# Wider transposes of the probabilities in a fused attention and gated-MLP kernel

## The chip, the cores and the metric

One Trainium2 chip, one of its NeuronCores. The metric is device time in microseconds (us) of one execution. Three runs of the kernel before gave 1160.24 us in the median (1160.02 to 1163.11).

## What is computed

The reference is local attention over 8 batches, 8 heads, 576 positions and 64 dimensions, followed by a gated MLP on 4608 tokens:

```python
scores = scale * np.matmul(q, k.transpose(0, 1, 3, 2))
masks = np.stack([mask_plain if h < H // 2 else mask_dil for h in range(H)], axis=0)
attn = softmax(np.where(masks, scores, -1e9))       # 32 keys back; heads 4 to 7: every 4th key, 128 back
x = np.matmul(attn, v)                              # (8 batches x 576) tokens x 512
xn = x / rms * rms_g
g = xn @ w_gate                                     # 512 -> 1536
out = (g * sigmoid(g) * (xn @ w_val)) @ w_out       # 1536 -> 512
```

## The kernel before, in words

The tokens are cut into 16 units of 288. A unit has 4 pairs of heads. In two of them the queries come in 3 blocks of 96 (QB); in the two dilated pairs they come in 4 blocks of 72, one for each residue class. So a unit has 14 blocks (a "burst" each), 6 with 96 queries and 8 with 72, and each block holds two heads.

A block passes through these steps, each on its own engine. PE multiplies queries and keys (`scored`, L452 in the first two units, L455 later). VectorE (DVE) adds the mask and takes the row maximum into the tile `t` (`scores_max`, L332 and L337). ScalarE (ACT) exponentiates in place (L347). DVE reduces and inverts the sums (L354, L355). GpSimd (POOL) scales the rows in place (L357; DVE for a part of unit 0). Then PE transposes the probabilities, once for each of the two heads (`transposed`, L429). In that transpose the probabilities are the stationary operand and an identity matrix of as many columns as the block has queries is the moving one: 96 or 72 columns. ACT and DVE take the result out of PSUM (`untranspose`, L412 and L414), and PE multiplies it with the values (`output`, L438, or L443 and L444).

The tile `t` comes from a rotating pool with 3 buffers under the tag "t". Every fourth block of the first two units takes a tile under the tag "qs" instead (L329, L330).

The transposed probabilities have no PSUM bank of their own. A bank holds 512 fp32 columns; the gate and value products of the MLP use 288 of them (U), and `gate` and `val` hand on the columns from U to U + 2*QB (L631, L657), and `products` takes them as `t_ps`.

The MLP runs over 12 slices (NJ) of the hidden size for every unit. One slice is three steps: the gate product (12 matmuls, L588 to L590, three for each of 4 chunks since both operands are split into a high and a low fp32r part), the value product (12 matmuls) and the projection of the slice before (12 matmuls). In units 0 and 1 the attention is in plain fp32, and unit 0 has its MLP in plain fp32 too (L585), while the weights are still decoded from fp64 bits on DVE and split (L152 to L162).

The order is written out by hand. `plan` puts each block's scores, transpose and output at a step of the main loop; in a step, PE first gets the MLP matmuls and then, by `attend`, the transposes, outputs and scores that fall on it. Work of the other engines is put off by a number of steps with a rank (`later`, `flush`). A unit's attention runs during the MLP of the unit before it. The transposes stand five steps after their block's scores, and the output two or three steps after the transpose. In the opening, before the first MLP step, each step also gets three or seven dummy matmuls (`busy`, L700).

At the very start POOL fills constants: the identity (`make_identity`), masks, sums (L97) and the zero halves of the first query and key tiles (L223).

Of the kernel before, what the change touches and what calls it, by code (L numbers as in the profile page):

```python
# [9 lines left out]
F32 = mybir.dt.float32  # L10
# [10 lines left out]
P = 128  # L21
U = S // 2
NU = NT // U
W = 32
DIL = 4
QB = 96
NC = DM // P
NJ = FF // P
NNAT = 2
# [35 lines left out]
def attn_moe(ctx: ExitStack, tc: tile.TileContext, qk_in, v_in, w_gate, w_val, w_out, rms_g, outT):  # L65
# [3 lines left out]
    nc = tc.nc  # L69
    V, A, G, PE = nc.vector, nc.scalar, nc.gpsimd, nc.tensor  # L70

    cst = ctx.enter_context(tc.tile_pool(name="cst", bufs=1))
    sb = ctx.enter_context(tc.tile_pool(name="sb", bufs=2))
    ps = ctx.enter_context(tc.tile_pool(name="ps", bufs=1, space=PSUM))


    ident = cst.tile([QB, QB], F32, name="ident")
    make_identity(nc, ident)
    one = cst.tile([P, 1], F32, name="one")
    G.memset(one, 1.0)  # L80
    ones = cst.tile([P, P], F32R, name="ones")
# [9 lines left out]
    G.affine_select(out=mask, in_=mask, pattern=[[1, P]], compare_op=ALU.is_ge,  # L91
                    fill=BIG, base=-1, channel_multiplier=-1)
    gs = cst.tile([P, NC], F32, name="gs")

    sums = [cst.tile([QB, 2, 4], F32, name=f"sum{k}") for k in range(5)]
    for sm in sums:
# [225 lines left out]

    st, xraw, xsq = {}, {}, {}

    def scores_max(u, c, i, s_ps):
        blocks, nq, _ = geometry(u, c)
        _, _, mc, n = blocks[i]
        sv = s_ps[:QB].rearrange("q (a t k) -> q a t k", a=2, t=2)
        other = u < NNAT and everything.index((u, c, i)) % 4 == 3  # L329
        t = sb.tile([QB, 2, P], F32, tag="qs" if other else "t", name=f"t_{u}_{c}_{i}", bufs=3)  # L330
        if u >= NNAT:
            V.tensor_tensor(out=t[:nq, :, :n], in0=sv[:nq, :, 1, :n],  # L332
                            in1=mask[:nq, None, mc:mc + n].to_broadcast([nq, 2, n]), op=ALU.add)
        sm = sums[everything.index((u, c, i)) % len(sums)]
        for a in range(2):
            plus = t[:nq, a, :n] if u >= NNAT else mask[:nq, mc:mc + n]
            V.tensor_tensor_reduce(out=t[:nq, a, :n], in0=sv[:nq, a, 0, :n], in1=plus,  # L337
                                   op0=ALU.add, op1=ALU.min, scale=-1.0 / math.sqrt(D),
                                   scalar=3e38, accum_out=sm[:nq, a, 0:1])
        st[u, c, i] = t, sm  # L340
# [75 lines left out]
    def products(q, t, o, t_ps, s_tag="s", o_tag="o"):  # L416


        if q:
            s_ps = ps.tile([P, 512], F32, tag=s_tag, name=f"s_{q[0]}_{q[1]}_{q[2]}")  # L420
        if o:
            o_ps = ps.tile([P, 512], F32, tag=o_tag, name=f"o_{o[0]}_{o[1]}_{o[2]}")
            pt = st.pop(o)
        if t:
            p, _ = st.pop(t)
        def transposed(a):
            blocks, nq, _ = geometry(*t[:2])
            n = blocks[t[2]][3]
            PE.transpose(t_ps[:n, a * QB:a * QB + nq], p[:nq, a, :n], ident[:nq, :nq])  # L429

        def output(a):
            blocks, nq, _ = geometry(*o[:2])
            n = blocks[o[2]][3]
            if a:
                return
            out = o_ps[:, :2 * nq].rearrange("d (a q) -> d a q", a=2)
            if o[0] < NNAT:
                PE.matmul(out, vs.pop(o)[:n].rearrange("k a d -> k (a d)"), pt[:n, 0, :, :nq], start=True, stop=True)  # L438
                return
            vh, vl = (part[:n].rearrange("k a d -> k (a d)") for part in vparts[everything.index(o) % 2])  # L440

            both = o_ps[:, :4 * nq].rearrange("d (t a q) -> d t a q", t=2, a=2)
            PE.matmul(both, vh, pt[:n, :, :, :nq], start=True, stop=False)  # L443
            PE.matmul(out, vl, pt[:n, 0, :, :nq], start=False, stop=True)  # L444

        def scored(a):
            blocks, nq, _ = geometry(*q[:2])
            qc, kc, _, n = blocks[q[2]]
            sv = s_ps[:QB].rearrange("q (a t k) -> q a t k", a=2, t=2)
            if q[0] < NNAT:  # L450
                qk = heads[q[0], 2 * q[1] + a]
                PE.matmul(sv[:nq, a, 0, :n], qk[:, qc:qc + nq], qk[:, U + kc:U + kc + n], start=True, stop=True)  # L452
                return
            qs, ks = heads[q[0], 2 * q[1] + a]
            PE.matmul(sv[:nq, a, :, :n], qs[:, qc:qc + nq], ks[:, :, kc:kc + n], start=True, stop=True)  # L455

        parts = [(b, fn, a) for b, fn in ((t, transposed), (o, output), (q, scored)) for a in range(2)]
        for b, fn, a in parts:
            if b:
                fn(a)  # L460
        if t:
            later(1, 0.2, lambda: untranspose(t, t_ps))
        if o:
            later(1, 0.5, lambda: take(*o, o_ps))
            if o[0] >= NNAT:
                later(1, 4, lambda: add(*o, o_ps))
            if o[0] < NNAT:
                later(1, 9, lambda: load_v(further(o, 3)))
            far = further(o, 2)
            if far and far[0] >= NNAT:  # L470
                split_v(far, 8 if o[0] < NNAT else 1)
        if q:
            later(1, 0.7, lambda: scores_max(*q, s_ps))
            later(2, 2, lambda: scores_exp(*q))
            later(3 if q[0] < NNAT else 4, -1, lambda: scores_norm(*q))
            u, c, i = q
            nxt = after(u, 2 * c, 2)
            nb = len(geometry(u, c)[0])
            if u < NNAT:
                if u == NNAT - 1 and c == NC - 1 and i == nb - 1:  # L480
                    for a in range(2):
                        later(1, 9, lambda a=a: load(NNAT, a))
                        later(5 + a, 9, lambda a=a: split(NNAT, a, (1, 2, 2, 3), G, V))
            elif nxt and i == 0:
                split(*nxt, (1, 2, 2, 3), G, V)
                split(nxt[0], nxt[1] + 1, (2, 3, 3, 4), G, V)
# [91 lines left out]
    hs, acc, gv = {}, {}, {}  # L578
# [30 lines left out]
    def gate(u, j):  # L609
        g_ps = group("g", u, j)  # L610
        if u == 0:
            used.append(("g", j))
        g = g_ps[:, :U]

        def tanh():
            nonlocal g
            t = (sb.tile([P, U], F32, tag="hhi", name=f"h_{j}", bufs=2) if u == 0 else
                 sb.tile([P, U], F32, tag="th", name=f"th_{u}_{j}", bufs=1))
            if u + j == 0:
                g = sb.tile([P, U], F32, tag="hhi", name="g_first", bufs=2)  # L620
                V.tensor_tensor(out=g, in0=g_ps[:, :U], in1=root[0], op=ALU.mult)
            A.activation(out=t, in_=g, func=AF.Tanh, scale=0.5)  # L622
            gv[u, j] = t

        def silu():
            t = gv[u, j]
            V.scalar_tensor_tensor(out=t, in0=t, scalar=1.0, in1=g, op0=ALU.add, op1=ALU.mult)  # L627

        later(1, 0 if u + j else 0.65, tanh)
        later(1, 0.8, silu)  # L630
        return g_ps[:, U:U + 2 * QB]  # L631

    def val(u, j):
        v_ps = group("v", u, j)
        if u == 0:
            used.append(("v", j))

        def prod():
            t = gv[u, j]
            V.tensor_tensor(out=t, in0=t, in1=v_ps[:, :U], op=ALU.mult)  # L640
            if u + j == 0:
                V.tensor_tensor(out=t, in0=t, in1=root[0], op=ALU.mult)

        def parts():
            t = gv.pop((u, j))
            if u == 0:
                hs[u, j] = t
                return
            hi = sb.tile([P, U], F32R, tag="hhi", name=f"hhi_{u}_{j}", bufs=2)
            lo = late[0].tile([P, U], F32R, tag="hlo", name=f"hlo_{u}_{j}", bufs=2)  # L650
            A.copy(out=hi, in_=t)  # L651
            G.tensor_tensor(out=lo, in0=t, in1=hi, op=ALU.subtract)  # L652
            hs[u, j] = (hi, lo)

        later(1 if u + j else 2, 0, prod)
        later(1 if u + j else 2, 0.5, parts)
        return v_ps[:, U:U + 2 * QB]  # L657

    def proj(u, j):
        if u == 0:  # L660
# [70 lines left out]
    for n in range(ends):  # L731
        decode(STEPS[n])
        flush()
        t_ps = None
        if "t" in events.get(n, {}):
            t_ps = ps.tile([P, 512], F32, tag="gv"[n % 2], name=f"t_first_{n}")[:, :2 * QB]
        attend(t_ps, s_tag=("s", "acc0", "acc1")[n % (3 if n < nb else 2)], o_tag=("o", "acc2")[n % 2])
        if n < nb + LAG:
            busy(BUSY[1])
        for kind, c in FIRST.get(n, ()):  # L740
            start(kind, c)
        if n == ends - 1:
            _, v_free = gate(0, 0), val(0, 0)
        now[0] += 1
# [101 lines left out]
```

## Time and profile before

| | us |
|---|---|
| median of 3 runs | 1160.24 |
| lowest and highest | 1160.02, 1163.11 |
| the profiled execution, its own time | 1162.36 |
| its span in the trace | 1160.6 |
| PE busy | 1125.2 (97%) |
| PE weight loads busy | 1088.5 (94%) |
| DVE, ACT, POOL busy | 798.8, 716.1, 611.5 |

The span is what the trace covers; 1.8 us of the profiled execution lie around it. PE is matmul, PEld the weight load that TensorE runs beside it. Matmuls are pipelined: the durations of neighbours overlap, so the pace of a stream is read from the distance of two starts, not from a duration.

### The profile page before, as it was taken

How to read it: one execution, taken by the hardware profiler on the slowest of the kernel's cores; microseconds unless marked ns; L12 is line 12 of the kernel's file. 1: busy time of each engine (PE TensorE's matmuls, PEld its weight loads, DVE VectorE, ACT ScalarE, POOL GpSimd, SP SyncE). 2: the span in 40 equal slices, each digit the busy share in tenths (PEclk: the TensorE clock that was granted, in tenths of full speed). 3: DMA queues.
4: the chain of work that ended last, by engine and by line, in shares of the span. 5: the costliest groups of instructions: out<-in, count | busy, mean ns of one | idle time of the engine just before them, and what ended most of it. 6: DMA issues, size and time to landing. Idle time of an engine off the chain costs nothing.

```text
span 1160.6 us, 25964 instructions
## 1 busy us (share of the span) xinstructions
PE 1125.2 (97%) x8357; PEld 1088.5 (94%) x8357; DVE 798.8 (69%) x2898; ACT 716.1 (62%) x2605; POOL 611.5 (53%) x1087
## 2 busy tenths in 40 slices
PE   8799788999999999999999999999999999999998
PEld 7577588999999999999999999999999999999998
DVE  5899777866758676675858767585776758586421
ACT  7476376675757567575666757576665757666311
POOL 6365344565546556564555655465565645565211
PEclk9899899999999999999999999999999999999999
DMA  8555221221213122131312213131221313120000
GB/s 245 156 210 179 76 75 39 80 61 31 82 37 103 39 70 62 35 86 34 95 41 81 58 31 90 31 101 40 71 61 35 95 33 91 38 81 15 1 21 22
DMA packets 61545, 82.19 MB, mean 71 GB/s; under 512 B 7298, under 2 KB 41090, under 8 KB 61410
## 3 DMA queue, kind: packets, MB, share of 16 engines
q1 hardware_dynamic: 61410, 80.54, 23.2%
q8 instruction: 67, 1.10, 0.4%
q14 instruction: 68, 0.56, 0.2%
HBM read 71.08 MB, written 9.44 MB: 69 GB/s over the span
## 4 chain that ended last, share of the span: by engine, by line
PE 75%; DVE 18%; issue 3%; ACT 2%; DMA 1%; POOL 0%; SPq 0%; POOLq 0%; DVEq 0%; ACTq 0%
PE acc L588 8%; PE acc L589 7%; PE acc L590 7%; PE g L588 7%; PE v L588 7%; PE g L590 7%; PE g L589 7%; PE v L589 7%; PE v L590 7%; DVE qs L315 3%; PE s L455 3%; PE o L443 3%; DVE t L337 2%; DVE xraw L551 2%; PE g L429 2%
## 5 line engine op out<-in xcount | busy, mean ns | idle before, releaser
L652 POOL TENSOR_TENSOR hlo<-th,hhi 128x288 fp32r<-128x288 f32 x180 | 144.8, 805 | 200.7 <-ACT hhi L651 196.9
L357 POOL TENSOR_SCALAR t<-t,sum 72x104 f32<-72x104 f32 (+3 forms) x442 | 165.7, 386 | 113.6 <-DVE sum L355 97.7
L590 PE MATMUL acc<-hhi,lo 128*128 128x288 f32 x720 | 212.1, 295 | 0.0
L590 PE MATMUL g<-xhi,lo 128*128 128x288 f32 x612 | 181.0, 296 | 0.0
L590 PE MATMUL v<-xhi,lo 128*128 128x288 f32 x612 | 180.3, 295 | 0.0
L651 ACT CAST hhi<-th 128x288 fp32r<-128x288 f32 x180 | 78.0, 433 | 163.7 <-DVE th L640 159.9
L347 ACT ACTIVATE t<-t,sum 96x128 f32<-96x128 f32 (+3 forms) x448 | 166.8, 375 | 12.3 <-DVE sum L337 11.4
L276 POOL TENSOR_TENSOR vlo<-vt,vhi 128x128 fp32r<-128x128 f32 x196 | 93.5, 477 | 122.7 <-ACT vhi L272 103.0
L387 DVE TENSOR_TENSOR xraw<-o,xraw 64x96 f32<-64x96 f32 (+1 forms) x392 | 106.8, 272 | 61.2 <-ACT xraw L377 56.4
L622 ACT ACTIVATE th<-g 128x288 f32<-128x288 f32 x180 | 73.8, 410 | 121.4 <-PE g L590 93.4
L590 PEld LDWEIGHTS acc<-hhi,lo 128*128 128x128 f32 x720 | 135.3, 188 | 0.0
L332 DVE TENSOR_TENSOR t<-s,mask 96x256 f32<-96x256 f32 (+3 forms) x196 | 71.7, 366 | 81.0 <-PE s L455 61.8
L627 DVE SCALAR_TENSOR_TENSOR th<-th,g 128x288 f32<-128x288 f32 x180 | 80.4, 447 | 68.0 <-ACT th L622 68.0
L590 PEld LDWEIGHTS g<-xhi,lo 128*128 128x128 f32 x612 | 115.5, 189 | 0.0
L590 PEld LDWEIGHTS v<-xhi,lo 128*128 128x128 f32 x612 | 115.1, 188 | 0.0
L588 PE MATMUL g<-xhi,hi_g 128*128 128x288 f32 x357 | 111.4, 312 | 0.6 <-DVE pt L414 0.5
L377 ACT COPY xraw<-o 64x96 f32<-64x96 f32 (+1 forms) x392 | 101.0, 258 | 16.1 <-PE o L444 13.8
L588 PE MATMUL acc<-hhi,hi_o 128*128 128x288 f32 x360 | 110.3, 306 | 0.0
L306 POOL TENSOR_TENSOR ks<-qk,ks 128x288 fp32r<-128x288 f32 (+2 forms) x112 | 107.4, 973 | 3.4 <-ACT ks L301 3.4
L589 PE MATMUL acc<-hlo,hi_o 128*128 128x288 f32 x360 | 106.6, 296 | 0.0
L640 DVE TENSOR_TENSOR th<-th,v 128x288 f32<-128x288 f32 x180 | 81.4, 452 | 36.2 <-PE v L590 33.2
L589 PE MATMUL g<-xlo,hi_g 128*128 128x288 f32 x322 | 95.4, 296 | 0.0
(173 smaller groups left out, 3569.7 us busy)
## 6 DMA issues: line engine op xcount, KB each, us to landing
qk<-in_qk_dram SPq DMA_DIRECT2D x60, 288.0 KB, 2.8
vt<-in_v_dram SPq DMA_DIRECT2D x196, 64.0 KB, 1.9
qk<-in_qk_dram SPq DMA_DIRECT2D x30, 352.0 KB, 3.0
out_dram<-ot SPq DMA_DIRECT2D x64, 144.0 KB, 1.9
qk<-in_qk_dram SPq DMA_DIRECT2D x30, 304.0 KB, 2.8
raw<-in_w_gate_dram SPq DMA_DIRECT2D x12, 512.0 KB, 4.3
raw<-in_w_val_dram SPq DMA_DIRECT2D x12, 512.0 KB, 4.0
raw<-in_w_out_dram SPq DMA_DIRECT2D x12, 512.0 KB, 4.2
```

Of the source, the lines that this page charges most:

```text
L276: G.tensor_tensor(out=vl, in0=vs.pop(b), in1=vh, op=ALU.subtract)
L306: ek.tensor_tensor(out=ks[:, 1, :nkt], in0=kr, in1=ks[:, 0, :nkt], op=ALU.subtract)
L347: A.activation(out=t[:nq, a, :n], in_=t[:nq, a, :n], func=AF.Exp, scale=-1.0, bias=sm[:nq, a, 0:1], accum_out=sm[:nq, a, 1:2])
L357: (V if u == 0 and (c, i) > (NC - 1, 0) else G).tensor_scalar(out=t[:nq, a, :n], in0=t[:nq, a, :n], scalar1=sm[:nq, a, 3:4], scalar2=1.0, ...
L377: A.copy(out=to[a * D:(a + 1) * D], in_=o[a * D:(a + 1) * D, (2 + a) * nq:(3 + a) * nq])
L387: V.tensor_tensor(out=to[rows], in0=o[rows, a * nq:(a + 1) * nq], in1=to[rows], op=ALU.add)
L588: PE.matmul(out, wh[:, cc, :], xh, start=start, stop=False)
L589: PE.matmul(out, wh[:, cc, :], xl, start=False, stop=False)
L590: PE.matmul(out, wl[:, cc, :], xh, start=False, stop=stop)
L627: V.scalar_tensor_tensor(out=t, in0=t, scalar=1.0, in1=g, op0=ALU.add, op1=ALU.mult)
L640: V.tensor_tensor(out=t, in0=t, in1=v_ps[:, :U], op=ALU.mult)
L652: G.tensor_tensor(out=lo, in0=t, in1=hi, op=ALU.subtract)
```

## The change

An identity of 112 rows and columns (WIDE) takes the place of the one of 96; its upper left 96 by 96 part still serves the other users. Three tiles of 112 rows are made once and set to zero at the start; the blocks take them in turn in place of pool tiles. A transpose then reads all 112 rows of such a tile, with the whole identity as the moving operand. Rows beyond the block's queries hold zeros or what an earlier block left there; the columns they give in PSUM are not read. The second head's result lies 112 columns behind the first in place of 96, which fills the bank (288 + 2*112 = 512). The 7 blocks of the first two units that use the tag "qs" keep their narrow transposes.

```diff
 QB = 96
+WIDE = 112
...
-    ident = cst.tile([QB, QB], F32, name="ident")
-    make_identity(nc, ident)
+    wide = cst.tile([WIDE, WIDE], F32, name="wide")
+    make_identity(nc, wide)
+    ident = wide[:QB, :QB]
...
+    probs = [cst.tile([WIDE, 2, P], F32, name=f"probs{k}") for k in range(3)]
+    for t in probs:
+        G.memset(t, 0.0)
+
     sums = [cst.tile([QB, 2, 4], F32, name=f"sum{k}") for k in range(5)]
...
+    def other(b):
+        return b[0] < NNAT and everything.index(b) % 4 == 3
+
     def scores_max(u, c, i, s_ps):
...
-        other = u < NNAT and everything.index((u, c, i)) % 4 == 3
-        t = sb.tile([QB, 2, P], F32, tag="qs" if other else "t", name=f"t_{u}_{c}_{i}", bufs=3)
+        k = everything.index((u, c, i))
+        t = (sb.tile([QB, 2, P], F32, tag="qs", name=f"t_{u}_{c}_{i}", bufs=3) if other((u, c, i)) else
+             probs[(k - k // 4 if u < NNAT else k) % len(probs)])
...
-            PE.transpose(t_ps[:n, a * QB:a * QB + nq], p[:nq, a, :n], ident[:nq, :nq])
+
+            rows = nq if other(t) else WIDE
+            PE.transpose(t_ps[:n, a * WIDE:a * WIDE + rows], p[:rows, a, :n], wide[:rows, :rows])
...
-        return g_ps[:, U:U + 2 * QB]
+        return g_ps[:, U:U + 2 * WIDE]
...
-        return v_ps[:, U:U + 2 * QB]
+        return v_ps[:, U:U + 2 * WIDE]
...
-            t_ps = ps.tile([P, 512], F32, tag="gv"[n % 2], name=f"t_first_{n}")[:, :2 * QB]
+            t_ps = ps.tile([P, 512], F32, tag="gv"[n % 2], name=f"t_first_{n}")[:, :2 * WIDE]
```

## Rows read from the trace of the kernel before

**Rows 1.** The page: engines' busy time (share, instructions); the chain that ended last, by engine.
```profile
PE 1125.2 (97%) x8357; PEld 1088.5 (94%) x8357; DVE 798.8 (69%) x2898; ACT 716.1 (62%) x2605; POOL 611.5 (53%) x1087
...
PE 75%; DVE 18%; issue 3%; ACT 2%; DMA 1%; POOL 0%; SPq 0%; POOLq 0%; DVEq 0%; ACTq 0%
```

**Rows 2.** Busy time by stretch: length, PE, PEld, DVE, ACT, POOL, granted clock, DMA.
```profile
10.00:20.00 10.00, 10.00 (x73) 8.54 (x72) 6.29 (x40) 8.75 (x36) 4.54 (x14) 1.00 1.06 301
50.00:150.00 100.00, 86.91 (x414) 68.76 (x415) 90.65 (x190) 61.56 (x180) 52.06 (x61) 0.93 0.43 148
150.00:200.00 50.00, 42.71 (x320) 40.12 (x319) 37.73 (x140) 35.61 (x128) 23.63 (x48) 1.00 0.22 64
200.00:1090.00 890.00, 887.04 (x6902) 880.37 (x6901) 619.53 (x2390) 574.73 (x2155) 496.96 (x900) 1.00 0.20 59
```

**Rows 3.** The same view of the transposes' line, L429, alone: PE and PEld.
```profile
200.00:1090.00 890.00, 56.51 (x364) 43.87 (x364) 1.00 0.20 59
```

**Rows 4.** Transposes by form: count, busy us (overlaps counted once), mean ns of one, idle before.
```profile
L429 PE MATMUL g<-ident,t 72*72 72x72 f32 x72 | 10.4, 225 | 1.5 <-DVE th L627 1.5
L429 PE MATMUL v<-ident,t 72*104 72x72 f32 x42 | 6.1, 225 | 0.0
L429 PE MATMUL v<-ident,t 96*128 96x96 f32 x30 | 5.0, 247 | 0.6 <-DVE th L640 0.6
```

**Rows 5.** Timeline, second transpose of a 96-column pair: start, duration, engine, line, tiles, count.
```profile
358.39 0.24 PE L429 MATMUL g<-ident,t 96*128 96x96 f32 x1
358.39 0.19 PEld L588 LDWEIGHTS v<-xhi,hi_g 128*128 128x128 f32 x1
...
358.50 0.19 PEld L589 LDWEIGHTS v<-spare,hi_g 128*128 128x128 f32 x1
```

**Rows 6.** Timeline, the second transpose of a 72-column pair.
```profile
602.15 0.22 PE L429 MATMUL g<-ident,t 72*72 72x72 f32 x1
602.15 0.19 PEld L588 LDWEIGHTS acc<-hhi,hi_g 128*128 128x128 f32 x1
...
602.26 0.19 PEld L589 LDWEIGHTS acc<-hlo,hi_g 128*128 128x128 f32 x1
```

**Rows 7.** Timeline: an fp32r product with 144 moving columns (L444) and its followers.
```profile
600.38 0.23 PE L444 MATMUL o<-pt,vlo 72*128 72x144 f32 x1
600.39 0.19 PEld L588 LDWEIGHTS v<-xhi,hi_g 128*128 128x128 f32 x1
600.45 0.34 PE L588 MATMUL v<-xhi,hi_g 128*128 128x288 f32 x1
600.50 0.19 PEld L589 LDWEIGHTS v<-xlo,hi_g 128*128 128x128 f32 x1
```

**Rows 8.** Plain fp32 with 288 columns: four matmuls in the timeline, and their group.
```profile
41.88 1.14 PE L585 MATMUL v<-xraw,f 128*128 128x288 f32 x4
...
L585 PE MATMUL v<-xraw,f 128*128 128x288 f32 x8 | 2.3, 405 | 0.0
```

**Rows 9.** Weight loads of 96-row transposes after 200 us: busy us, mean ns of one, idle before.
```profile
L429 PEld LDWEIGHTS g<-ident,t 96*128 96x128 f32 x104 | 12.8, 141 | 5.9 <-issue 5.4
```

**Rows 10.** Evacuations of the transposes on ACT, by form.
```profile
L412 ACT CAST pt<-g 128x192 fp32r<-128x192 f32 x55 | 17.4, 317 | 20.5 <-PE g L429 16.2 <-DVE sum L354 4.3
L412 ACT CAST pt<-g 104x144 fp32r<-104x144 f32 x35 | 9.7, 276 | 19.2 <-PE g L429 12.4 <-DVE xraw L387 6.9
```

**Rows 11.** POOL at the start, timeline; and two of its memsets by form.
```profile
2.32 7.34 POOL L223 MEMSET qk<- 64x576 f32 x13
9.77 2.17 POOL L357 TENSOR_SCALAR t<-t,sum 96x96 f32<-96x96 f32 x6
...
L223 POOL MEMSET qk<- 64x576 f32 x5 | 2.6, 572 | 0.1
L223 POOL MEMSET qk<- 64x704 f32 x4 | 2.6, 680 | 0.0
```

**Rows 12.** Timeline of the opening: a decode step that waited for its DMA.
```profile
17.38 1.17 ACT L152 ACTIVATE f<-raw 128x1024 f32<-128x1024 f32 x1 [0.21 <-DMA raw<-in_w_val_dram]
```

## The prediction

> **What bounds the kernel now.** The page comes first: PE is busy for 1125.2 of 1160.6 us, and the chain that ended last runs 75% over PE and 18% over DVE [rows 1]. A share over the whole span mixes stages, so the table by stretch comes next [rows 2]. From 200 to 1090 us PE is busy for 887.04 of 890.00 us at a granted clock of 1.00, its upper level (2.4 GHz); DVE, the next busiest, has 619.53. There PE's own stream sets the time, and what is added to that stream is added to the end. From 50 to 150 us DVE has 90.65 of 100 us and PE 86.91, so PE has holes there, as from 150 to 200 us (42.71 of 50). From 10 to 20 us PE is full, but partly with the dummy matmuls.
>
> So the question is what a transpose takes of PE's stream. Counting them first: 364 lie between 200 and 1090 us [rows 3], two for each block, so 182 pairs; the other 42 of the 16 x 14 blocks come before. The 182 are 13 units' worth at 6 blocks of 96 and 8 of 72: 78 and 104 pairs.
>
> **What a pair takes today.** Durations of matmuls overlap. But the pair's busy time counts the overlap once, so that less the mean of one is the distance of the two starts, which is what the first transpose takes of the stream. For 96 columns: 5.0 us / 15 pairs = 333 ns, less 247, is 86 ns. For 72: 6.1 / 21 = 290, less 225, is 65; the third form gives 10.4 / 36 = 289, less 225, 64 [rows 4]. Both 72-column forms agree although one loads 104 weight columns and the other 72: the number of weight columns does not matter, the moving columns do. 24 more cost 21 ns, 0.87 ns each. Plain fp32 with 288 columns fits: four take 1.14 us and the last of them about 0.405, so (1.14 - 0.405) / 3 = 245 ns, 0.85 ns for each column [rows 8].
>
> The second transpose behaves differently. The load of the next matmul's weights starts with it (358.39, 602.15) and the load behind that one 0.11 us later (358.50, 602.26), whether the moving operand has 96 columns or 72 [rows 5, 6]. An fp32r product with 144 columns shows the same 0.11 us between the loads (600.39, 600.50), although its own stream is over after 0.07 (600.38 to 600.45) [rows 7]. So behind a short matmul the stream waits for the 128-column load: 110 ns, and a transpose shorter than that costs 110 all the same.
>
> **The change, part by part.** *First transpose of a pair.* With 112 columns at 0.87 ns it takes 86 + 16 x 0.87 = 100 ns in place of 86, and 100 in place of 65 for 72 columns: 14 and 35 ns more. No row shows a transpose with 112 columns. From below I bound it by the 0.49 ns for each column of the fp32r product (0.07 us / 144), 54 ns in all; from above by plain fp32's 0.85, which gives 95, and the slope of 0.87 from 96, which gives 100. The last is nearest, since it is the same operation and only 16 columns away. 78 x 14 + 104 x 35 = 1.1 + 3.6 = **4.7 us**, all in the stretch where PE is full.
>
> *Second transpose.* 100 ns still fit into the 110 of the load: nothing. If that cover were gone, it would cost the same 4.7 us once more.
>
> *Weight loads of the transposes.* They have 112 rows in place of 96 or 72, but as many columns as before. The one with 96 rows by 128 columns lasts 141 ns [rows 9] where the MLP's load of 128 rows by 128 columns lasts 0.19 us [rows 5], so there is room, and they run beside the MLP matmul ahead or the first transpose: nothing.
>
> *Evacuation.* ACT and DVE read as many elements as before, 112 columns apart. The 72-column blocks are read with gaps already: 276 ns for 144 elements against 317 for 192 without gaps [rows 10], so gaps have no price that shows. Nothing.
>
> *Lasting tiles.* The pool had three buffers, and there are three tiles. The mask step of the third block after waits for the same transpose as before; blocks are about two steps apart and the transpose stands five steps after its scores, so it is over before. Neither DVE nor POOL gets a new wait, SP's queue no new instruction.
>
> *Start.* POOL gets three memsets of 256 elements. Two existing ones give (680 - 572) / 128 = 0.84 ns for each element, so 572 - 320 x 0.84 = 303 ns each, 0.9 us in all. They stand ahead of 7.34 us of memsets without a hole, right behind which POOL scales the first blocks (9.77) [rows 11]. The first transpose therefore comes up to 0.9 us later. The dummies leave no hole to make it good from 10 to 20 us [rows 2], but ACT's decode step at 17.38 waits for a DMA that doesn't move [rows 12], and work up to it can slip without cost. Ends 0 and 0.9; I take 0.4, halfway.
>
> *Transposes before 200 us.* 7 of the 42 pairs stay narrow; 35 pairs at some 26 ns (the mean of 14 and 35 by 6 and 8) are 0.9 us at most. PE has 7 to 13 us of holes in each of these stretches [rows 2], and DVE is the busier in the first. Ends 0 and 0.9; I take 0.2.
>
> **Sum:** 4.7 + 0.4 + 0.2 = 5.3 us. On the profiled execution, 1162.36 us with 1.8 us outside its span, that makes 1167.7. That execution is itself 2.1 us above the median of the runs shown, so for the median I forecast 1160.24 + 5.3 = **1165.5 us**, 0.46% slower.
>
> **Rivals.** *A: a wide transpose streams faster for each column.* If 112 columns went at the fp32r product's 0.49 ns, the first transpose would need 54 ns. For that its partner's weights must be in by then: that load lasts 141 ns [rows 9] where one that paces the stream at 110 lasts 190, so by estimate some 61 ns for 128 columns. So about 61 against 86 and 57 against 65: 78 x 25 + 104 x 8 = 2.8 us gained, 1160.24 - 2.8 + 0.6 = 1158.0. If PE's remaining holes in this stretch (890 - 887 = 3.0 us) closed as well, 1155.0. Against it: 72 and 96 columns lie on one line with plain fp32, with no sign of a faster form. The Trainium skill has a rule for it: "TensorE: Matmul & The Clock Gate", Terms, says that the transpose mode makes FP32 four times faster. Here a transposed column costs as much as a plain fp32 one, 0.87 and 0.85 ns, so on the moving side the trace does not agree.
>
> *B: the added columns are cheap.* The rows can't rule out that part of the step from 72 to 96 goes with the 24 more rows of both operands. If the columns alone cost 0.49 ns, 40 x 0.49 = 20 and 16 x 0.49 = 8 ns: 104 x 20 + 78 x 8 = 2.7 us, 1163.5; if they cost nothing, 1160.8. Both count as no change. Against it: plain fp32 has the same slope at 128 rows. The same page's section on the back-to-back issue gap has a warm matmul take N / 2.4 + 2.5 ns; by that the estimate is 104 x 16.7 + 78 x 6.7 = 2.3 us. The trace has twice that slope for fp32 operands.
>
> *C: the cover of the second transpose fails,* because the next load starts later or needs the array that the wide one holds. Then the 4.7 us come twice: 1170.2. It decides as soon as the second transpose with its overhead exceeds 110 ns. Against it: the load starts in the same 10 ns as the transpose.
>
> **How the numbers follow.** A measurement of this kernel tells some 0.3% (3.5 us) from no change: below 1156.8 is faster, above 1163.7 slower. The forecast gets 0.62; its own range is 1163.4 (no cost at the start and 0.85 ns for each column, less 0.9 of spread) to 1168.5 (all upper ends, and the three runs' spread of up to 3 us in part); 0.05 of it falls within 0.3%. A gets 0.18, of which 0.12 is beyond the bound; B 0.13, all within; C 0.07. So faster 0.12, same 0.05 + 0.06 + 0.13 = 0.24, slower 0.57 + 0.07 = 0.64. The range leaves out A alone (0.18): from 1159.8, which is B's lower end less 1.0 for the runs, to 1170.5, which takes in C.
>
> **What would show it.** In the profile after, a pair's busy time less the mean of one should give about 100 ns for all forms; the two weight loads behind the second transpose should still be 0.11 us apart; the stretch in which PE is full should be about 4.7 us longer; POOL's first L357 should start near 10.7 us. The forecast is wrong if that distance stays at 65 to 86 ns or falls to 60 (B, A), or if the loads behind lie more than 0.11 us apart (C). If the distance is 100 ns and the time does not rise, then the stream was not the bound from 200 to 1090 us, and the first step of this working is what failed.

## The result and the profile after

The changed kernel takes 1167.68 us in the median of 7 runs (1165.57 to 1169.15), the kernel before 1162.48 us in the 7 runs that it now has (1160.02 to 1165.05). The ratio is 1.0040, with a 95% interval of 1.0026 to 1.0054: slower by some 5 us. The profiled execution after took 1167.75 us with a span of 1166.0.

Busy times and instruction counts come first, from the page of the kernel after. They answer to [rows 1].

```profile
PE 1133.5 (97%) x8357; PEld 1097.2 (94%) x8357; DVE 798.9 (69%) x2898; ACT 716.9 (61%) x2605; POOL 613.4 (53%) x1090
```

PE has the same 8357 matmuls and is busy 8.3 us longer; POOL has three more instructions, the memsets; DVE and ACT are as before. Next the transposes by form, from the view of lines (count, busy us, mean ns of one, idle before). They answer to [rows 4]; the line is now L441.

```profile
L441 PE MATMUL g<-wide,probs 112*72 112x112 f32 x72 | 12.8, 259 | 1.4 <-DVE th L639 1.4
L441 PE MATMUL v<-wide,probs 112*104 112x112 f32 x42 | 7.5, 259 | 0.0
L441 PE MATMUL v<-wide,probs 112*128 112x112 f32 x30 | 5.4, 260 | 0.5 <-DVE th L652 0.5
```

Read as in the prediction, the distance of the two starts of a pair is 12.8 / 36 - 0.259 = 97 ns, 7.5 / 21 - 0.259 = 98 and 5.4 / 15 - 0.260 = 100. All three forms have come to the same price, whether they had 64, 65 or 86 before. The timeline of one pair whose block has 72 queries answers to [rows 6]:

```profile
469.41 0.36 PE L441 MATMUL g<-wide,probs 112*72 112x112 f32 x2
469.51 0.19 PEld L600 LDWEIGHTS acc<-hhi,hi_g 128*128 128x128 f32 x1
469.62 0.19 PEld L601 LDWEIGHTS acc<-hlo,hi_g 128*128 128x128 f32 x1
...
469.51 0.26 PE L441 MATMUL g<-wide,probs 112*72 112x112 f32 x1
```

The second transpose still starts together with the load behind it (469.51), and the load after that comes 0.11 us later (469.62), as in [rows 5, 6]. The second transpose got wider for nothing; the first pays.

Where the 5 us lie is seen from landmarks. The first matmul for the row norms of a unit (L495, after the change L507) stands at the same place in PE's stream of every unit. From the third unit's to the last one's lie 13 units. Timeline rows, first of the kernel before, then of the kernel after:

```profile
207.45 0.42 PE L495 MATMUL rps<-inv,sq 128*96 128x2 f32 x4
1085.66 0.42 PE L495 MATMUL rps<-inv,sq 128*96 128x2 f32 x4
```

```profile
208.27 0.42 PE L507 MATMUL rps<-inv,sq 128*96 128x2 f32 x4
1091.08 0.42 PE L507 MATMUL rps<-inv,sq 128*96 128x2 f32 x4
```

The 13 units take 1085.66 - 207.45 = 878.21 us before and 1091.08 - 208.27 = 882.81 after: **4.60 us more**, where the prediction's sum for them was 4.7. What follows the last landmark is 1160.6 - 1085.7 = 74.9 before and 1166.0 - 1091.1 = 74.9 after. The stretch ahead of the first is 0.8 us longer, but the experiments show how little that says.

The trace allows the same count pair by pair. Added up over the 182 pairs after 200 us, the distances from a first transpose to its second grow from 14.17 to 18.65 us: 4.48 of the 4.60. The forms above do not show all of them. In 34 pairs, 20 with 96 columns and 14 with 72, the first weight load came late, 30 or 31 ns ahead of its matmul and after an idle time of 70 ns or more. Their distances are 109 to 114 and 78 to 81 ns before, 122 to 124 and 112 to 114 after. So they are longer in both kernels, and the change adds some 12 and 33 ns to them as well.

PE's waits in the stretch did not change. PE is busy for 887.26 of 890 us where it was 887.04 [rows 2], and from 200 to 1085 us its longest entry is the wait of transposes for DVE's sums, 2.1 us in 8 waits, before as after:

```profile
200.00:1090.00 890.00, 887.26 (x6866) 881.01 (x6865) 619.58 (x2386) 573.66 (x2151) 495.64 (x897) 1.00 0.20 59
...
PE g L429 <- DVE sum L354: 2.1, 8, 0.3
...
PE g L441 <- DVE sum L364: 2.1, 8, 0.3
```

The start came as worked out, only smaller. In POOL's timeline after, the three memsets take 0.26 us (1.67 to 1.93) and twice 0.25 (2.17 to 2.67) where 0.303 was worked out, and the first scaling starts at 10.50 in place of 9.77 [rows 11]:

```profile
1.67 0.31 POOL L99 MEMSET probs<- 112x256 f32 x1
1.93 0.29 POOL L93 TENSOR_SCALAR_AFFINE_SELECT mask<-mask 96x128 f32<-96x128 f32 x1
2.17 0.56 POOL L99 MEMSET probs<- 112x256 f32 x2
2.67 0.24 POOL L103 MEMSET sum<- 96x8 f32 x5
...
10.50 2.06 POOL L367 TENSOR_SCALAR probs<-probs,sum 96x96 f32<-96x96 f32 x6
```

Less of it reaches PE. Its first transposes, before and after, start 0.34 us apart:

```profile
10.86 0.33 PE L429 MATMUL t_first<-ident,t 96*96 96x96 f32 x2
...
11.20 0.36 PE L441 MATMUL t_first<-wide,probs 112*96 112x112 f32 x2
```

### The profile page after: what moved, and what is told of

It reads as the page before. It is cut to its first block, busy times and chain, and to the rows that moved or that the text cites. A ratio compares the mean times of both kernels' runs of the same rounds, so it can differ in the third digit from the quotient of the medians.

```text
span 1166.0 us, 25946 instructions
## 1 busy us (share of the span) xinstructions
PE 1133.5 (97%) x8357; PEld 1097.2 (94%) x8357; DVE 798.9 (69%) x2898; ACT 716.9 (61%) x2605; POOL 613.4 (53%) x1090
## 4 chain that ended last, share of the span: by engine, by line
PE 78%; DVE 17%; issue 2%; ACT 2%; POOL 0%; POOLq 0%; DVEq 0%; ACTq 0%
PE acc L600 8%; PE acc L601 7%; PE acc L602 7%; PE g L600 7%; PE v L600 7%; PE g L601 7%; PE g L602 7%; PE v L601 7%; PE v L602 7%; DVE qs L321 3%; PE s L467 3%; PE o L455 2%; PE g L441 2%; DVE xraw L563 2%; DVE probs L347 2%
## 5 line engine op out<-in xcount | busy, mean ns | idle before, releaser
L367 POOL TENSOR_SCALAR probs<-probs,sum 96x128 f32<-96x128 f32 (+3 forms) x430 | 158.2, 380 | 96.0 <-DVE sum L365 89.0
L357 ACT ACTIVATE probs<-probs,sum 96x128 f32<-96x128 f32 (+3 forms) x434 | 161.5, 375 | 12.5 <-DVE sum L347 11.5
L342 DVE TENSOR_TENSOR probs<-s,mask 96x256 f32<-96x256 f32 (+3 forms) x196 | 71.7, 366 | 83.0 <-PE s L467 56.7
```

The source lines that it names most:

```text
L357: A.activation(out=t[:nq, a, :n], in_=t[:nq, a, :n], func=AF.Exp, scale=-1.0, bias=sm[:nq, a, 0:1], accum_out=sm[:nq, a, 1:2])
L367: (V if u == 0 and (c, i) > (NC - 1, 0) else G).tensor_scalar(out=t[:nq, a, :n], in0=t[:nq, a, :n], scalar1=sm[:nq, a, 3:4], scalar2=1.0, ...
```

## The experiments

The theory: a short matmul costs PE's stream its own columns (0.83 to 0.87 ns each in a transpose) or the weight load behind it, whichever is longer; 110 ns was read for an MLP load of 128 columns. The rivals: both transposes of a pair pay a share; the price has a jump; the lasting tiles bring waits of their own.

The first four take the changed kernel and alter the one line that sets how many rows a transpose takes. They ran together, 5 rounds, with the kernel before at 1162.91 us.

**Only the first transpose wide.**

```diff
-            rows = nq if other(t) else WIDE
+            rows = nq if other(t) or a == 1 else WIDE
```

> Only the first transpose of a pair takes 112 rows and columns; the second keeps 96 or 72. Theory (the first pays by its columns, the second is covered by the 110 ns weight load behind it): first start to second start about 99 ns in all forms, the loads behind the second still 0.11 us apart, and the whole cost of the change stays: some 4.6 us over the 13 units from 200 to 1090 us, the ratio near 1.004. Rival (each of the two wide transposes pays a share): half of it, 2.3 us, the ratio near 1.002.

Measured: 1167.61 us, ratio 1.0043 (1.0029 to 1.0057). The landmarks of its trace:

```profile
208.07 0.42 PE L507 MATMUL rps<-inv,sq 128*96 128x2 f32 x4
1090.83 0.42 PE L507 MATMUL rps<-inv,sq 128*96 128x2 f32 x4
```

882.76 us for the 13 units, 4.55 more than before. The whole cost is there with half of the widening.

**Only the second transpose wide.**

```diff
-            rows = nq if other(t) else WIDE
+            rows = nq if other(t) or a == 0 else WIDE
```

> Only the second transpose of a pair is wide. Theory: the distance of the two starts stays at 85 and 65 ns, the 110 ns of the load behind cover the wide one, and the 13 units cost nothing; at most the 0.4 us of the three memsets remain, a ratio of 1.000 to 1.0005. Rival (both pay): 2.3 us, near 1.002. Rival C (the cover fails): the loads behind lie over 0.11 us apart.

Measured: 1162.83 us, ratio 1.0001 (0.9990 to 1.0012). Its landmarks, and a pair of its timeline:

```profile
206.48 0.42 PE L507 MATMUL rps<-inv,sq 128*96 128x2 f32 x4
1084.49 0.42 PE L507 MATMUL rps<-inv,sq 128*96 128x2 f32 x4
...
984.15 0.33 PE L441 MATMUL g<-wide,probs 72*72 72x72 f32 x2
984.22 0.19 PEld L600 LDWEIGHTS acc<-hhi,hi_g 128*128 128x128 f32 x1
984.33 0.19 PEld L601 LDWEIGHTS acc<-hlo,hi_g 128*128 128x128 f32 x1
```

878.01 us for the 13 units, nothing more than before. The first start to the second is 0.07 us again, and the two loads are 0.11 us apart with 112 columns streaming under the first of them. The rival of a shared price and the prediction's C are out.

**The tiles, the memsets and the spacing in PSUM alone,** all transposes narrow.

```diff
-            rows = nq if other(t) else WIDE
+            rows = nq
```

> The three lasting tiles, their memsets and the spacing of 112 in PSUM stay, but every transpose is as narrow as before. Theory: the 13 units take what they took before (rounded to 0.2 us), the first transpose starts 0.3 us later, and the time is that of before within 0.5 us, a ratio of 1.000. Rival (lasting tiles or the gap in PSUM bring waits, or take some away): the 13 units are longer or shorter by 1 us or more.

Measured: 1162.97 us, ratio 0.9998 (0.9987 to 1.0009). Landmarks:

```profile
209.30 0.42 PE L507 MATMUL rps<-inv,sq 128*96 128x2 f32 x4
1087.28 0.42 PE L507 MATMUL rps<-inv,sq 128*96 128x2 f32 x4
```

877.98 us. The tiles bring no waits to the 13 units. The first landmark says more: 209.30 here and 206.48 in the run before, although both have the same memsets and tiles. The opening varies by 2.8 us from one execution to the next, so one profile can't tell the prediction's 0.6 us for the start and the early transposes from nothing. The interval of this ratio allows up to 1.0 us.

**All of them 96 rows and columns.**

```diff
-            rows = nq if other(t) else WIDE
+            rows = nq if other(t) else QB
```

> All these transposes take 96 rows and columns, so only the blocks of 72 are widened, by 24 columns. Theory (0.83 to 0.87 ns for each column of the first transpose): 104 pairs by 20 to 21 ns, 2.1 us over the 13 units, a ratio near 1.002. Rival (a price that jumps somewhere above 96 columns and not below): the 13 units take what they took before.

Measured: 1165.08 us, ratio 1.0015 (1.0004 to 1.0026). Landmarks:

```profile
208.31 0.34 PE L507 MATMUL rps<-inv,sq 128*96 128x2 f32 x3
1088.73 0.42 PE L507 MATMUL rps<-inv,sq 128*96 128x2 f32 x4
```

880.42 us, 2.21 more than before: 2210 / 104 = 21 ns for 24 columns. The full change adds 4600 - 2210 = 2390 ns for the step from 96 to 112 on 182 pairs, 13 ns for 16 columns. That is 0.88 and 0.82 ns for a column: one line, no jump. Since the identity is square, rows and columns of these transposes could not be changed apart, so no run shows which of the two sets the price.

The other eight runs ask whether the cover of the second transpose is really the load behind it, and whether a pair can be made cheaper that way. If a load of 72 or 96 columns stands behind it in place of 128, a narrow one should cost less than 110 ns, and a wide one should no longer be free. The scores have such loads, so transposes must stand directly ahead of scores. All of these move a step from the fourth unit on, where blocks are two steps apart.

**Transposes one step later, ahead of scores; then the same with wide ones; one step earlier; and a control with the old order.**

```diff
-        t_at, o_at = [t + 5 for t in q_at], [t + 8 for t in q_at]
+        t_at, o_at = [t + (6 if u > NNAT else 5) for t in q_at], [t + 8 for t in q_at]
...
-        parts = [(b, fn, a) for b, fn in ((t, transposed), (o, output), (q, scored)) for a in range(2)]
+        parts = [(b, fn, a) for b, fn in (((o, output), (t, transposed), (q, scored)) if t and t[0] > NNAT else
+                                        ((t, transposed), (o, output), (q, scored))) for a in range(2)]
```

The second run has the same edit on the changed kernel, the third 4 in place of 6, the control the first line alone.

> The kernel before with its narrow transposes; from the fourth unit on (those whose blocks are two steps apart) the transposes stand one step later, in the step of another block's scores, and PE gets outputs, transposes, scores in this order. Behind the second transpose then stands a load of 96 or 72 columns in place of one of 128. Theory (a short matmul costs its own stream or the load behind it, whichever is longer): 110 ns become 86 for the 6 blocks of 96 and 65 for 5 of the 8 blocks of 72 (the last three of a unit have no scores beside them): 6 x 24 + 5 x 45 = 0.37 us for each unit, 4.8 us less over 13 units, a ratio near 0.996. Rival (the 110 ns are a fixed cost behind a transpose): no gain, 1.000. If the output, now two steps behind its transpose in place of three, waits for the evacuation, part of the gain goes into PE's waits at the output.

> The changed kernel, wide transposes, with the same new places and order as the run before it. Theory: the cover of the second transpose is smaller here (some 80 and 62 ns of load behind it where it was 110), so width is paid twice: 4.6 us for the first and 6 x 14 + 5 x 34 = 0.25 us for each unit, 3.3 us over 13 units, for the second; 7.9 us longer than the narrow one in the same order, 3 us or so longer than the kernel before. Rival (the second wide transpose is always free): 4.6 us longer than the narrow one in the same order.

> As the first of these runs, but the transposes stand one step earlier than before in place of one later, so that four steps lie between transpose and output. Theory: the same 4.8 us less, if the normalised probabilities are there in time; each wait for POOL's scaling before a transpose takes from it. Rival (fixed cost): no gain.

> A control: the transposes one step later as in the first of these runs, but PE gets transposes, outputs, scores in the old order, so that a load of 128 columns stands behind the second transpose as before. Theory: the second transpose costs its 110 ns again and the 13 units take what they took before, a ratio of 1.000. Rival (moving the step alone brings the gain or the loss): the same time as the first of these runs.

Measured, with the kernel before at 1163.08 us: 1206.88 (ratio 1.0375, 1.0353 to 1.0397), 1210.95 (1.0414, 1.0393 to 1.0435), 1236.53 (1.0641, 1.0616 to 1.0667) and 1209.94 us (1.0402, 1.0382 to 1.0421). All are misses as a whole: moving the step costs 40 us and more, with the old order too. The first run's table by stretch (columns as in [rows 2]), and below it PE's waits from 200 to 1130 us (for whom, us in total, times, longest):

```profile
200.00:1100.00 900.00, 873.45 (x6653) 846.14 (x6653) 592.68 (x2326) 555.26 (x2095) 485.06 (x875) 0.95 0.19 58
```

```profile
PE v L589 <- DVE pt L414: 12.1, 21, 0.8
PE g L429 <- DVE th L628: 7.2, 26, 0.3
PE o L443 <- DVE xraw L387: 5.8, 20, 0.3
```

PE, which had 3.0 us of holes in 890, has 26.6 in 900. It waits for DVE: for the evacuation of a transpose before the next value product, for the gate step before a transpose, for the addition of an output before the next output. The third run, one step earlier, also waits for POOL's scaling, 12.8 us in 33 waits.

PE's row shows only about half of the 43.8 us lost, because the recorded durations of neighbours overlap and cover short waits. The row of the weight loads shows the rest: they are busy for 846.14 of 900 us where they were busy for 880.37 of 890 [rows 2], so their holes grew from 9.6 to 53.9 us, about what was lost.

DVE was not busier over the stretch, 592.68 of 900 us where it was 619.53 of 890 [rows 2]. But it stood idle ahead of its part of the evacuation (L414), which waits for ACT's part (L412). From 200 to 1085 us, before and in the first run:

```profile
DVE pt L414 <- ACT pt L412: 22.7, 46, 0.8
...
DVE pt L414 <- ACT pt L412: 182.9, 136, 2.7
```

So the evacuation came later than the work that waited for it. Which of the moved pieces of work made it late was not tried.

The control shows what stands behind the price of the second transpose. There the load of the output's weights follows it in 169 of the 182 pairs. That load has 72 to 128 rows, but always 128 columns:

```profile
603.58 0.29 PE L429 MATMUL v<-ident,t 72*72 72x72 f32 x2
603.65 0.19 PEld L443 LDWEIGHTS o<-pt,vhi 72*128 72x128 f32 x1
603.76 0.19 PEld L444 LDWEIGHTS o<-pt,vlo 72*128 72x128 f32 x1
```

The loads are 0.11 us apart here too (108 to 110 ns in all 169). So the 110 ns do not belong to the MLP's matmuls, and the rows of the load do not count.

**Scores one step earlier,** so that they stand behind transposes that keep their place, on the kernel before and on the changed one.

```diff
         t_at, o_at = [t + 5 for t in q_at], [t + 8 for t in q_at]
+        if u > NNAT:
+            q_at = [t - 1 for t in q_at]
```

> The kernel before, narrow transposes; from the fourth unit on the scores are issued one step earlier, so that they stand right behind the transposes of another block, while transposes and outputs keep their steps. Theory: the second transposes fall to 86 and 65 ns as above (0.37 us for each unit), but the outputs now stand alone, and their second matmul (88 or 67 ns of stream) meets a load of 110 ns that it did not meet: 6 x 22 + 4 x 43 = 0.30 us for each unit. Net 0.07 us for each unit, 0.9 us less over 13 units, a ratio of 0.999, if no new waits come. Rival (any move of a step brings waits, as with the moved transposes): 10 us or more longer.

> The changed kernel with the scores one step earlier in the same way. Theory: the wide second transpose takes its own 99 ns in place of 86 or 65 there, so widening costs 4.6 us for the first and 3.3 us for the second, 7.9 us over 13 units against the run before it. Rival: 4.6 us.

Measured: 1205.16 us (1.0359, 1.0339 to 1.0379) and 1210.86 us (1.0408, 1.0391 to 1.0426), the kernel before at 1163.19. The rival's 10 us or more is what came. But the pairs that didn't wait show the price itself. Timeline of the narrow kernel, then of the wide one: a pair, the two scores loads behind its second transpose together, and the second of these loads by itself.

```profile
593.41 0.29 PE L429 MATMUL v<-ident,t 72*72 72x72 f32 x2
593.48 0.21 PEld L455 LDWEIGHTS s<-ks,qs 128*72 128x72 f32 x2
...
593.54 0.14 PEld L455 LDWEIGHTS s<-ks,qs 128*72 128x72 f32 x1
```

```profile
597.35 0.36 PE L441 MATMUL v<-wide,probs 112*72 112x112 f32 x2
597.45 0.24 PEld L467 LDWEIGHTS s<-ks,qs 128*72 128x72 f32 x2
...
597.54 0.14 PEld L467 LDWEIGHTS s<-ks,qs 128*72 128x72 f32 x1
```

Behind the narrow one the loads are 0.06 us apart (593.48, 593.54), not 0.11. Behind the wide one they are 0.09 apart (597.45, 597.54). This holds for every such pair after 200 us: with 72 queries and a 72-column load behind, 61 to 64 ns in the 65 pairs of the narrow run and 95 to 96 in the 65 of the wide one. The 39 pairs that still have a 128-column load behind them keep 108 to 110 ns in both runs. So the cover was the 128-column load: with a shorter one in its place, the second transpose pays for its width too. Whether the narrow one's 61 to 64 ns are its own 65 or the 72-column load (110 x 72 / 128 = 62 by estimate) can't be told apart here.

The times do not show it in full. Over 13 units the wide kernel takes 4.1 us more than the narrow one here and 5.4 in the pair of runs above, where the theory had 7.9 and its rival 4.6. Taken alone, these sums would speak for the rival. The two runs by stretch, over their 13 units (columns as in [rows 2]), show where the rest went, the narrow one first:

```profile
205.46:1126.52 921.06, 893.93 (x6810) 868.56 (x6809) 614.95 (x2372) 568.14 (x2133) 490.50 (x892) 1.00 0.19 57
208.03:1133.18 925.15, 901.31 (x6811) 876.43 (x6809) 615.00 (x2372) 568.40 (x2133) 493.58 (x892) 1.00 0.19 57
```

The weight loads are busy for 7.9 us more (868.56, 876.43), as the theory has it, and idle for 3.8 us less (52.5, 48.7): the longer stream filled waits that were there anyway. In the pair of runs above it is 7.3 us more and 2.0 less.

**Only the late blocks.** To keep the gain without the waits, the last two move only the transposes of the 72-column blocks, in the order outputs, transposes, scores, and with the transposes last.

```diff
-        t_at, o_at = [t + 5 for t in q_at], [t + 8 for t in q_at]
+        t_at, o_at = [t + (6 if u > NNAT and k > 5 else 5) for k, t in enumerate(q_at)], [t + 8 for t in q_at]
```

> The kernel before; only the transposes of the 72-column blocks, from the fourth unit on, stand one step later, in the step of scores, with the order outputs, transposes, scores. Theory: 5 of these 8 pairs fall from 110 to 65 ns in their second transpose, 0.22 us for each unit, 2.9 us less over 13 units, if the transposes find DVE in time; where they wait for DVE's step on the gate (L627), 0.1 to 0.2 us each, the gain is eaten and the time is 1163 or more. Rival (the moved step as such costs some 40 us): 1200 us.

> As the run before it, but in the order outputs, scores, transposes, so that the transposes come some 0.2 us later and a load of 128 columns stands behind them again. Theory: the wait for DVE goes or shrinks; the second transpose costs 110 ns as before, while the second scores matmul, with a transpose's short load behind it, loses its own stall of 12 or 43 ns: 5 pairs by some 27 ns, 0.14 us for each unit, 1.8 us less over 13 units at best. Rival: the same waits as in the run before it, and no gain.

Measured: 1169.43 us (1.0057, 1.0041 to 1.0074) and 1171.72 us (1.0081, 1.0060 to 1.0101), the kernel before at 1163.03. The waits ate more than the gain in both: the 13 units are 6.6 and 8.5 us longer than before, and in them the weight loads are idle for 17.3 and 18.8 us where it was 9.5. The rival's 1200 us did not come. The loads' waits of the first, from 200 to 1090 us; the first row was there before (5.4 us in 13 waits), the others are new:

```profile
PEld g L429 <- issue: 5.5, 14, 0.5
PEld g L429 <- DVE th L628: 3.0, 14, 0.3
PEld v L589 <- DVE pt L414: 2.8, 13, 0.2
```

No version that beats the kernel before was found.

## Why the prediction was right

**The bound** was read rightly: in the stretch from 200 to 1090 us PE's stream is full, and 4.60 us put into it came out at the end as 4.60 between the landmarks, with no wait of PE closing or opening.

**The first transpose** was said to go from 86 and 65 to 100 ns; it went to 97 to 100, and the sum of 4.7 us came out as 4.60, of which the distances of the pairs show 4.48. The run with the first alone gives 4.55. The prediction took the price of pairs whose loads were in time for all; 34 pairs cost more, but more in both kernels, so the sum was not touched. Of the two bounds, the line through 72 and 96 columns was the right one to carry on; the fp32r product's 0.49 ns for each column would have made the change a gain.

**The second transpose** was costed at nothing, with the load of the next MLP weights named as its cover and C as what follows without it. The run with the second alone costs nothing, and the runs with a shorter load behind it show it paying, so the cover is shown. The point from which C decides, a transpose of more than 110 ns ahead of a 128-column load, was not run.

**Weight loads, evacuation, lasting tiles:** nothing, as costed; the run with the tiles and the spacing alone takes 877.98 us for the 13 units, and the one with the second transposes wide 878.01, weight loads of 112 rows included.

**Start and early transposes,** 0.4 and 0.2 us: the mechanism at the start is there (POOL 0.73 us late, where 0.9 was worked out, and PE's first transpose 0.34), but whether it reaches the end stays open, below what these runs tell.

**Rival A** fell to the first form table after: 97 to 100 ns, where it had 57 to 61. The Trainium skill ("TensorE: Matmul & The Clock Gate", Terms) says that the transpose mode makes FP32 four times faster. At 112 columns, too, no row shows that on the moving side; the profile lists these transposes as MATMUL and does not tell their mode.

**Rival B** (cheap columns) fell to the same table and to the run with 96 columns everywhere, 21 ns for 24 columns. Its condition, that a part of the price goes with the rows, is not refuted, since every run changed both. But it could not have given B's price either: the change adds rows along with the columns, which the prediction overlooked.

**The number:** 5.3 us more were forecast and 1167.68 - 1162.48 = 5.2 measured. That they agree so closely is partly luck: the interval of the ratio reaches from 3.0 to 6.3 us, and of the 5.3 only the 4.7 are borne out by landmarks. That the forecast said 1165.5 and not 1167.7 is due to the base: the three runs shown had a median 2.2 us below that of seven.

## What to carry to other kernels

Between long matmuls, a short one cost its own columns here or the weight load behind it, whichever was longer; so look at what stands behind it before paying to shorten it, or before believing that lengthening it is free. Here the second of each pair had 45 or 25 ns to spare and the first had none, so one width for both was free for the second and paid by the first. What a load costs is read from the trace and not from its columns alone: the second transpose's own weights can have 128 columns too, yet their load (141 ns recorded, where the MLP's has 190 [rows 5, 9]) does not hold the first transpose above its 85 to 87 ns when it starts in time. A hole of 45 ns in a hand-written order is not worth moving a step for, unless the engines that feed that step have room there. And PE's waits are better read from the row of its weight loads than from that of its matmuls, which showed about half of them.

## What the runs showed beyond that

The spread of this kernel's runs goes with the mean granted clock, which dips only in the opening 200 us (0.93 from 50 to 150 us and 1.00 from 150 to 1090 in the kernel before [rows 2]): among the runs of the kernel before that stood beside the experiments, the 9 with a mean of 0.996 or 0.997 took 1160.14 to 1161.46 us, and the 8 with 0.990 took 1164.41 to 1166.13. That is nearly what the change costs, and it is the reason for comparing landmarks. That the dips cause it was not tried.

In the first of the moved runs the granted clock is recorded as 0.95 from 200 to 1100 us, neither of the two levels seen elsewhere. Yet its stream goes at the old pace. PE's timeline there:

```profile
700.17 0.29 PE L589 MATMUL v<-xhi,hi_v 128*128 128x288 f32 x1
700.31 0.29 PE L590 MATMUL v<-spare,hi_v 128*128 128x288 f32 x1
700.44 0.29 PE L591 MATMUL v<-xhi,lo 128*128 128x288 f32 x1
```

The starts are 0.13 us apart, as in the kernel before (600.63 to 600.76 there), and the same kernel's other runs, with means of 0.990 to 0.993 where this one has 0.941, took 1205.02 to 1208.59 us against its 1207.55. Whether the record or the stream is the exception was not tried.
